# A recurrent attention and four-expert kernel: the first group's first layer in f32r parts for three of its four experts

## The chip, the cores and the metric

The kernel runs on one core of a Trainium2 chip. The metric is the device time of one execution in microseconds (us); the time before is the median of three runs. A profile is one more execution, with its own time.

## The reference

Two blocks follow each other. The first is a gated linear recurrence per batch and head, with 4 batches, 8 heads, 768 steps and head size 48; the second multiplies each of the 3072 tokens (384 values) by four experts' two layers and adds the results with normalised weights.

```python
for t in range(S):
    state = alpha[:, :, t, :, None] * state + np.einsum('bhd,bhe->bhde', k[:, :, t], v[:, :, t])
    y[:, :, t] = np.einsum('bhd,bhde->bhe', q[:, :, t], state)
...
x = np.ascontiguousarray(attn_out.transpose(0, 2, 1, 3)).reshape(B * S, H * D)
...
p = domain_probs / (domain_probs.sum(-1, keepdims=True) + 1e-09)
for e in range(E):
    h = np.maximum(x @ w1[e], 0.0)
    out += p[:, e:e + 1] * (h @ w2[e])
```

All data are float32. w1 is 384 x 1024 and w2 1024 x 384 for each of the four experts.

## The kernel before, in words

**Units and groups.** The sequence is cut into six blocks of 128 steps. A block of one batch is a unit, 24 in all; a unit's attention yields 128 tokens of x. Units are gathered into groups (L117): the first group has two units (256 tokens), four groups have four, the last has two. For each group the experts' layers run one expert after the other (`tasks`, L119): `up` is the first layer, one call for each of the eight 128-wide hidden tiles (called fc 0 to 7 below), `down` the second layer, and `add_up` (L863) weights and sums.

**f32 and f32r.** TensorE takes a plain float32 product in several passes, an f32r product in one, at less precision. From the second group on each operand of a product is therefore split into three f32r parts (a rounded top, a sum and a rest scaled up), and a product is three f32r products, one for each part. For w1 and w2 this is `split_piece` (L241): ACT makes the top part, DVE the two others (L250, L252, L253), and POOL's queue writes all three to DRAM (`kept`, L256), from where later groups load them (L214). A weight matrix of an expert is cut into four such pieces, so pieces 0 to 3 belong to the first expert, 4 to 7 to the second, and so on. For x it is `split_x` (L720): ACT makes the top of all three 128-row slices in step 0, DVE the two other parts of one slice in each of the steps 1 to 3.

**The first group** does not use parts. Its `up` multiplies the plain f32 x by the plain f32 w1 (L769), with the relu on ACT (L771); its `down` is plain f32 too (L847, 16 matmuls of each expert for each of the two units). Its raw x lies in the third part of the tile xT (L446 and L667). Beside that, the pieces of w1 are split for the later groups: for the second to fourth expert two pieces are queued at the start of one of the calls of `down` of the expert before (L814), the two others after the hidden tiles 2 and 4 of its own `up` (`SPLIT_AT`, L203). The first expert runs in two halves of 128 tokens, since the second unit's x comes later.

**Background and order.** `background` (L258) issues the steps of queued splits: a top part on ACT, at the next call its DVE operations. The order on every engine is thus the order in which the program text issues things. The attention of coming units runs beside the layers as a generator that is stepped at times that a planner deals out (`deal`, L895); `advance` (L944) adds the estimated cost of each layer's step (`cost`, L889) to a clock and steps what is due.

**A unit's steps** that the prediction speaks of: transposes on TensorE (tp, L287) with their copies on ACT (L494 and L502); L507, L508 and L520 on DVE; then seven levels, of which each has copies of q on ACT (qb, L541), products of q, decay and k on DVE (L548, L550, L560) and a copy of k on ACT (L559); near (L593); score products on TensorE (sc, L567) and masked copies on DVE (L577); the far products (L623) with their copies (L636); lat (L640); yps (L662), which gives x (copied by L675); and the state (sps, L697; L705 to L708).

The tile pools set when buffers come free: the parts of w1 have four buffers (`AHEAD`, L200), so the fourth next piece waits until the older one's write to DRAM has been done and its readers are through.

Of the kernel before, what the change touches and what calls it, by code (L numbers as in the profile page):

```python
# [20 lines left out]
def kernel(  # L21
# [37 lines left out]
    nc = tc.nc  # L59

    B, H, S, D = q.shape
    E, DM, F = moe_w1.shape
    P = 128
# [5 lines left out]
    KC = DM // P  # L69
    FCH = F // P  # L70
    NT = B * P
    NQ = 4
# [74 lines left out]
    hidden = {}  # L147
    finish = deque()
    making = deque()
    splitting = []  # L150
    stores = deque()
    late = deque()
# [47 lines left out]
    AHEAD = 4  # L200


    SPLIT_AT = [{1: 2, 4: 3}, {1: 0, 3: 1, 5: 2, 7: 3}]  # L203
    BESIDE = [{2: 0, 3: 1, 4: 2, 5: 3}, {1: 2, 2: 3}]

    def load_piece(l, i, beside=False):
# [34 lines left out]
    def split_piece(l, i):  # L241
        gi, k = divmod(i, E * NQ)
        whole = wt[l][i]
        if i >= E * NQ:
            w = wt[l][i] = wts.tile([P, 3, KC * QF], F32R, name="w2", bufs=NQ)
        else:
            w = wts.tile([P, 3, KC * QF], F32R, name="w1", bufs=AHEAD)
        top, both, rest = (w[:, part] for part in range(3))

        nc.scalar.activation(out=top, in_=whole, func=ACT.Copy, scale=LIFT)  # L250
        yield
        nc.vector.tensor_sub(rest, whole, top.bitcast(F32))  # L252
        nc.vector.scalar_tensor_tensor(out=both, in0=rest.bitcast(F32), scalar=4096.0, in1=whole,  # L253
                                       op0=ALU.mult, op1=ALU.add)
        if (gi, k // NQ) != (1, 0):
            nc.gpsimd.dma_start(out=kept[l][k], in_=w.bitcast(F32))  # L256

# [32 lines left out]
    def first_unit(fill, other):  # L290
# [153 lines left out]
        flat_v = rv.rearrange("p h d -> p (h d)")  # L444
        work.tile([P, 96], F32, name="space", bufs=1)
        xTs[0] = work.tile([P, 3, KC, NT], F32R, name="xT", bufs=1)  # L446
        xraws[0] = xTs[0][:, 2].bitcast(F32)
        terms = [[] for _ in range(P // QUAD)]
        for c in range(KC):
            for j, strip in enumerate(terms):  # L450
# [9 lines left out]
            nc.scalar.copy(out=xraws[0][:, :, HALF * s:HALF * (s + 1)], in_=y)  # L460
        next_k(6)
        return rest_of_first(AT, KTs[6], rv)

    def rest_of_first(AT, KT, rv):
        nc.scalar.copy(out=AT, in_=turned(lambda p: KT[:, p, :]))
        yield
        sps = ps.tile([P, NP, 2, D], F32, name="sps", tag="w")
        for p in range(NP):
            nc.tensor.matmul(sps[:, p], lhsT=AT[:, p], rhs=rv[:, 2 * p:2 * p + 2, :D], start=True, stop=True)
        for i in range(2):  # L470
            rows = slice(HD * i, HD * (i + 1))
            nc.vector.tensor_copy(out=sts[units[0][1]][rows, :, i, :], in_=sps[rows, :, i, :])
        load(2, "v")
        yield

    def attention(u):
# [171 lines left out]
        def result():  # L648
            yps = ps.tile([P, KC, P], F32, name="yps", tag="w")
            strips = [[] for _ in range(P // QUAD)]  # L650
            for c in range(KC):
                for j, strip in enumerate(strips):
                    p, part = divmod(len(strips) * c + j, 3)
                    terms = [(flat_st[:, p, QUAD * part:QUAD * (part + 1)], QT[:, p, :])] if cb > 0 else []
                    for i in range(2):
                        if part != 2 * (1 - i):
                            at = VD * (2 * p + i) + QUAD * part - D * i
                            terms.append((flat_v[:, at:at + QUAD], lat[:, 2 * p + i, :]))
                    strip += [(c, n == 0, n == len(terms) - 1, *term) for n, term in enumerate(terms)]
            for turn in zip(*strips):  # L660
                for j, (c, begins, ends, lhsT, rhs) in enumerate(turn):
                    nc.tensor.matmul(yps[QUAD * j:QUAD * (j + 1), c, :], lhsT=lhsT, rhs=rhs,  # L662
                                     start=begins, stop=ends)
            gi, slot = place[cb, b]
            if slot == 0:
                if gi == 0:
                    xTs[gi] = work.tile([P, 3, KC, NT], F32R, name="xT", bufs=1)  # L667
                    xraws[gi] = xTs[gi][:, 2].bitcast(F32)
                elif gi < LAST:
                    xraws[gi] = work.tile([P, KC * NT + PAD], F32, name="x_raw", bufs=1)[:, :KC * NT]  # L670
                    xraws[gi] = xraws[gi].rearrange("p (c n) -> p c n", n=NT)
                else:
                    xraws[gi] = []
            if gi < LAST:
                nc.scalar.copy(out=xraws[gi][:, :, slot * P:(slot + 1) * P], in_=yps)  # L675
            else:

                xraws[gi].append(AT)
                nc.scalar.copy(out=AT[:, :KC, :], in_=yps)
# [33 lines left out]
    def x_part(gi, part, kc):  # L713
        n = len(groups[gi]) * P
        if gi < LAST:
            return xTs[gi][:, part, kc, :n]
        t, i = divmod(part * KC + kc, NP * P // n)
        return xTs[gi][t].rearrange("p a n -> p (a n)")[:, i * n:(i + 1) * n]

    def split_x(gi, step):  # L720

        n = len(groups[gi]) * P
        if step == 0 and gi < LAST:
            xTs[gi] = work.tile([P, 3, KC, NT], F32R, name="xT", bufs=1)
        elif step == 0:

            xTs[gi] = [work.tile([P, NP, P], F32R, name="KT", bufs=5) for _ in range(5)]
        for kc in range(KC) if step == 0 else [step - 1]:
            parts = [x_part(gi, part, kc) for part in range(3)]
            pieces = [(xraws[gi][:, kc, :n], parts)] if gi < LAST else                 [(raw[:, kc, :], [part[:, s * P:(s + 1) * P] for part in parts])  # L730
                 for s, raw in enumerate(xraws[gi])]
            for x, out in pieces:
                if step == 0:
                    nc.scalar.activation(out=out[0], in_=x, func=ACT.Copy, scale=TRIM)
                else:
                    split_rest(x, out)


    def up(gi, e, fc, slots=None):
# [17 lines left out]
            for k in range(NQ):  # L757
                load_piece(0, (e + 1) * NQ + k)
        col = slice(f * P, (f + 1) * P)
        if gi > 0:  # L760
            w = wt[0][i].rearrange("p t (c f) -> p t c f", f=QF)[:, :, :, col]
        else:
            w = wt[0][i].rearrange("p (c f) -> p c f", f=QF)[:, :, col]
        parts = [hidden[c][:, part, f, lo:hi] for part in range(3)]
        whole = parts[2].bitcast(F32)
        one = ps.tile([P, NT], F32, name="one", tag="g", bufs=4)[:, :hi - lo]
        if gi == 0:
            for kc in range(KC):
                nc.tensor.matmul(one, lhsT=w[:, kc], rhs=xraws[gi][:, kc, lo:hi],  # L769
                                 start=(kc == 0), stop=(kc == KC - 1))  # L770
            nc.scalar.activation(out=whole, in_=one, func=ACT.Relu)  # L771
        else:
            for part in (1, 2, 0):
                for kc in range(KC):
                    nc.tensor.matmul(one, lhsT=w[:, part, kc], rhs=x_part(gi, part, kc),  # L775
                                     start=(part == 1 and kc == 0), stop=(part == 0 and kc == KC - 1))
            nc.scalar.activation(out=parts[0], in_=one, func=ACT.Relu, scale=TRIM)  # L777
            while finish:
                hidden_rest(*finish.popleft())
            finish.append((one, parts))  # L780
# [27 lines left out]
    def down(gi, e, slots, between):  # L808
# [2 lines left out]
        first = first_piece(gi, e)  # L811
        tiles = range(FCH)
        if gi == 0 and e < E - 1 and slots[0] == (e == 0):
            making.extend(split_piece(0, first + NQ + k) for k in range(2))  # L814
        if gi == 0 and e == E - 1 and slots[0] == 1:
            making.extend(split_piece(1, first + NQ + k) for k in range(NQ // 2))
        while fresh(gi, e) and (making or splitting):
# [71 lines left out]
    def cost(layer, gi, e):  # L889
        n = len(groups[gi]) / 4  # L890
        if layer == 0:
            return 2.1 * n if gi > 0 else 2.6 * n
        return 4.1 if gi > 0 else 5.4

    def deal():  # L895
# [54 lines left out]
    with tc.manual_schedule():  # L950
# [46 lines left out]
        for (gi, e), after in zip(tasks, [*tasks[1:], (None, None)]):  # L997
            rest = gi == e == 0
            for fc in range(FCH):
                up(gi, e, fc, slice(1, len(groups[0])) if rest else None)  # L1000
                advance(cost(0, gi, e) / (2 if rest else 1))
            each = len(groups[gi]) if gi > 0 else 1
            turns = [range(k, k + each) for k in range(rest, len(groups[gi]), each)]
            for k, slots in enumerate(turns):

                between = deque()
                if after[1] == 0:

# [36 lines left out]
```

## Time and profile before

| | us |
|---|---|
| median of three runs | 1033.85 (1030.1 to 1035.3) |
| profiled execution, its own time | 1027.61 |
| its span, first to last instruction | 1025.7 |
| TensorE matmul busy | 998.4 (97%) |
| DVE busy | 702.4 (68%) |
| ACT busy | 438.7 (43%) |
| first group's first layer, TensorE (L769) | 46.2 in 240 passes, 20.4 to 145.0 |

The time of the profiled execution holds the span and a little around it. Busy time counts an engine's instructions, with matmul ends modelled. The chain of waits goes back from the last instruction to what released each step, and so names what ended last in each stretch. A group of instructions is given as line, engine, operation and tiles; L769 appears twice as often as the program issues it, since a plain f32 matmul is recorded as two. Stretches list the busy time of each engine between two times.

### The profile page before, as it was taken

The page shows a single profiled execution, that of the slowest core. Times are in us where ns is not written, and L with a number is a line of the kernel's source. Part 1 is how long each engine was busy: PE and PEld are TensorE (multiplying, and loading weights), DVE is VectorE, ACT ScalarE, POOL GpSimd, SP SyncE. Part 2 cuts the span into 40 slices and gives each one's busy share as a digit, 9 for nine tenths or more (in the row PEclk, how much of TensorE's full clock was granted, in tenths as well). Part 3 has the DMA queues.
Part 4 walks back from the last instruction along what each step waited for, and adds up shares of the span by engine and source line. Part 5 has one row for each costly group of instructions (what it writes and reads, how often), then busy time and mean ns, then how long its engine had stood idle before and what let it go on. Part 6 is the DMA issues. An engine that isn't in the chain of part 4 may idle for free.

```text
span 1025.7 us, 21120 instructions
## 1 busy us (share of the span) xinstructions
PE 998.4 (97%) x8564; PEld 886.7 (86%) x8564; DVE 702.4 (68%) x1430; ACT 438.7 (43%) x961; POOL 36.1 (4%) x79
## 2 busy tenths in 40 slices
PE   8889999999999999999999999999999999999998
PEld 7667777988888799898898898888988989898998
DVE  5698879687979868677767666885877743434343
ACT  5687666365354444335443415444454332211111
POOL 2010000000000100000000000000000000000000
PEclk9999999999999999999999999999999999999999
DMA  9499699398988999789889759786796454454531
GB/s 214 135 387 282 201 359 338 107 337 265 322 284 249 317 296 330 284 253 317 287 259 334 235 214 385 263 274 261 212 365 250 170 205 184 185 195 174 221 149 47
DMA packets 155632, 260.19 MB, mean 254 GB/s; under 512 B 95216, under 2 KB 132464, under 8 KB 133520
## 3 DMA queue, kind: packets, MB, share of 16 engines
q1 hardware_dynamic: 149072, 216.44, 63.7%
q0 software_dynamic: 6016, 42.08, 10.2%
q8 instruction: 68, 1.11, 0.4%
q10 hardware_dynamic: 448, 0.33, 0.1%
q14 instruction: 28, 0.23, 0.1%
HBM read 216.35 MB, written 42.47 MB: 252 GB/s over the span
## 4 chain that ended last, share of the span: by engine, by line
PE 81%; DVE 11%; ACT 4%; issue 2%; DMA 0%; POOL 0%; DVEq 0%; SPq 0%; ACTq 0%; POOLq 0%
PE ops L847 35%; PE one L775 31%; PE sc L567 5%; PE yps L662 3%; PE one L769 2%; PE tp L287 2%; DVE w L252 2%; ACT qb L541 2%; DVE hT L805 1%; DVE hT L800 1%; DVE near L577 1%; DVE QT L548 1%; PE sps L697 1%; DVE w L253 1%; PE far L623 1%
## 5 line engine op out<-in xcount | busy, mean ns | idle before, releaser
L847 PE MATMUL ops<-w,hT 128*128 128x384 f32 x2112 | 381.8, 339 | 9.4 <-ACT hT L777 6.7
L847 PEld LDWEIGHTS ops<-w,hT 128*128 128x128 f32 x2112 | 366.4, 189 | 15.6 <-ACT hT L777 8.9
L775 PE MATMUL one<-xT,w 128*128 128x512 f32 x1440 | 342.8, 394 | 0.8 <-DVE acc L875 0.8
L775 PEld LDWEIGHTS one<-xT,w 128*128 128x128 f32 x1440 | 266.8, 188 | 58.3 <-DVE acc L875 1.2
L777 ACT ACTIVATE hT<-one 128x512 fp32r<-128x512 f32 (+1 forms) x192 | 107.9, 562 | 343.4 <-PE one L775 318.7
L800 DVE SCALAR_TENSOR_TENSOR hT<-one,hT 128x512 fp32r<-128x512 f32 (+1 forms) x192 | 122.3, 645 | 105.2 <-ACT hT L777 104.8
L541 ACT COPY qb<-QT 64x256 f32<-64x256 f32 x322 | 131.1, 407 | 88.7 <-DVE QT L518 44.9
L548 DVE TENSOR_TENSOR QT<-QT,AT 128x256 f32<-128x256 f32 x158 | 66.7, 422 | 85.9 <-ACT qb L541 85.1
L805 DVE SCALAR_TENSOR_TENSOR hT<-hT 128x512 fp32r<-128x512 f32 (+1 forms) x192 | 112.8, 640 | 0.1
L577 DVE COPY_PREDICATED near<-masks,sc 128x256 f32<-128x256 uint8 x138 | 73.9, 536 | 41.5 <-PE sc L567 38.1
L567 PEld LDWEIGHTS sc<-qb,KT 128*64 128x64 f32 x2208 | 69.7, 138 | 7.3 <-issue 5.7
L567 PE MATMUL sc<-qb,KT 128*64 128x64 f32 x2208 | 74.0, 223 | 0.9 <-ACT qb L541 0.9
L875 DVE SCALAR_TENSOR_TENSOR acc<-ops,p_all,acc 128x384 f32<-128x384 f32 x66 | 40.0, 614 | 42.8 <-PE ops L847 42.8
L560 DVE TENSOR_TENSOR KT<-KT,AT 128x256 f32<-128x256 f32 x161 | 67.4, 418 | 0.0
L559 ACT COPY KT<-KT 128x256 f32<-128x256 f32 x138 | 57.5, 416 | 3.3
L769 PE MATMUL one<-xT,w 128*128 128x256 f32 (+1 forms) x240 | 46.2, 340 | 0.4 <-ACT xT L460 0.4
L847 PE MATMUL ops<-hT 128*128 128x384 f32 x128 | 46.2, 494 | 0.0
L550 DVE TENSOR_TENSOR AT<-AT 128x256 f32<-128x256 f32 (+1 forms) x138 | 39.1, 284 | 4.7
L769 PEld LDWEIGHTS one<-xT,w 128*128 128x128 f32 x240 | 37.7, 191 | 4.9 <-ACT xT L460 0.6
L884 POOL DMA_DIRECT2D out_dram<-acc x22 | 11.9, 540 | 673.7 <-DVE acc L875 673.7
L662 PE MATMUL yps<-lat,rv 128*32 128x128 f32 x736 | 33.1, 273 | 1.6 <-ACT lat L640 1.6
L775 PE MATMUL one<-KT,w 128*128 128x256 f32 x288 | 34.6, 279 | 0.0
(119 smaller groups left out, 709.1 us busy)
## 6 DMA issues: line engine op xcount, KB each, us to landing
w<-kept SPq DMA_DIRECT2D x140, 1152.0 KB, 8.8
kept<-w POOLq DMA_DIRECT2D x32, 1152.0 KB, 8.7
hT<-in_moe_w_dram SPq DMA_DIRECT2D x36, 384.0 KB, 5.9
w<-in_moe_w_dram SPq DMA_DIRECT2D x16, 384.0 KB, 5.8
rv<-in_v_dram SPq DMA_DIRECT2D x24, 192.0 KB, 9.3
out_dram<-acc POOLq DMA_DIRECT2D x22, 192.0 KB, 6.4
rk<-in_k_dram SPq DMA_DIRECT2D x14, 192.0 KB, 6.1
rq<-in_q_dram SPq DMA_DIRECT2D x14, 192.0 KB, 3.0
```

The source lines that it names most:

```text
L541: nc.scalar.copy(out=qb[rows, :, i, :].rearrange("p a (b r) -> p a b r", r=m), in_=qv[rows])
L548: nc.vector.tensor_mul(qv, qv, spread(dv[:, :, :, 0], m))
L560: nc.vector.tensor_mul(new[:, :, :, 0, :], old[:, :, :, 0, :], spread(halved(decs[li])[:, :, :, 1], m))
L567: nc.tensor.matmul(out[HALF * s:HALF * (s + 1), 2 * p:2 * p + 2, :], lhsT=KTs[li][:, p, HALF * s:HALF * (s + 1)], rhs=qbs[li][:, p, :, QUA ...
L577: nc.vector.copy_predicated(near.rearrange("p a (b two r) -> p a b two r", two=2, r=m)[:, :, :, 1, :], mk.unsqueeze(1).broadcast_to([P, H, ...
L662: nc.tensor.matmul(yps[QUAD * j:QUAD * (j + 1), c, :], lhsT=lhsT, rhs=rhs, start=begins, stop=ends)
L769: nc.tensor.matmul(one, lhsT=w[:, kc], rhs=xraws[gi][:, kc, lo:hi], start=(kc == 0), stop=(kc == KC - 1))
L775: nc.tensor.matmul(one, lhsT=w[:, part, kc], rhs=x_part(gi, part, kc), start=(part == 1 and kc == 0), stop=(part == 0 and kc == KC - 1))
L777: nc.scalar.activation(out=parts[0], in_=one, func=ACT.Relu, scale=TRIM)
L800: nc.vector.scalar_tensor_tensor(out=low, in0=x, scalar=0.0, in1=top.bitcast(F32), op0=ALU.max, op1=ALU.subtract)
L805: nc.vector.scalar_tensor_tensor(out=dif, in0=low.bitcast(F32), scalar=-4096.0, in1=top.bitcast(F32), op0=ALU.mult, op1=ALU.add)
L847: nc.tensor.matmul(sums[slot], lhsT=h, rhs=w, start=(n == begins[slot]), stop=(n == ends[slot]))
```

## The change

In the first group, the first layer of the second, third and fourth expert is computed in three f32r parts like that of the later groups. Raw x lies in a tile of its own (`x_raw`), and is split into the three parts of xT beside the second unit's call of `down` of the first expert; the parts begin 16 elements into their rows (`SHIFT`). The parts of w1 are read from the tiles in which `split_piece` makes them (`ready`), and `up` issues background steps until its piece has been issued. Three pieces instead of two are queued at the start of `down`, and the fourth after the first hidden tile of `up`. The relu still makes the whole f32 hidden value on ACT. The planner's cost of such a layer is lowered from 2.6 to 2.1 for a full group.

```diff
-    SPLIT_AT = [{1: 2, 4: 3}, {1: 0, 3: 1, 5: 2, 7: 3}]
+    SPLIT_AT = [{0: 3}, {1: 0, 3: 1, 5: 2, 7: 3}]
+    SHIFT = 16
...
+        if i < E * NQ and l == 0:
+            ready[i] = w
...
-        xraws[0] = xTs[0][:, 2].bitcast(F32)
+        xraws[0] = x_raw()
...
+    def x_raw():
+        t = work.tile([P, KC * NT + PAD], F32, name="x_raw", bufs=1)
+        return t[:, :KC * NT].rearrange("p (c n) -> p c n", n=NT)
...
-                if gi == 0:
-                    xTs[gi] = work.tile([P, 3, KC, NT], F32R, name="xT", bufs=1)
-                    xraws[gi] = xTs[gi][:, 2].bitcast(F32)
-                elif gi < LAST:
-                    xraws[gi] = work.tile([P, KC * NT + PAD], F32, name="x_raw", bufs=1)[:, :KC * NT]
-                    xraws[gi] = xraws[gi].rearrange("p (c n) -> p c n", n=NT)
-                else:
-                    xraws[gi] = []
+                xraws[gi] = x_raw() if gi < LAST else []
...
-            return xTs[gi][:, part, kc, :n]
+            return xTs[gi][:, part, kc, SHIFT * (gi == 0):][:, :n]
...
-        if gi > 0:
-            w = wt[0][i].rearrange("p t (c f) -> p t c f", f=QF)[:, :, :, col]
+        in_parts = gi > 0 or e > 0
+        if in_parts and gi == 0:
+            while i not in ready:
+                background()
+        if in_parts:
+            w = (wt[0] if gi > 0 else ready)[i].rearrange("p t (c f) -> p t c f", f=QF)[:, :, :, col]
...
-        if gi == 0:
+        if not in_parts:
             for kc in range(KC):
                 nc.tensor.matmul(one, lhsT=w[:, kc], rhs=xraws[gi][:, kc, lo:hi],
                                  start=(kc == 0), stop=(kc == KC - 1))
-            nc.scalar.activation(out=whole, in_=one, func=ACT.Relu)
...
-            making.extend(split_piece(0, first + NQ + k) for k in range(2))
+            making.extend(split_piece(0, first + NQ + k) for k in range(3))
...
-            return 2.1 * n if gi > 0 else 2.6 * n
+            return 2.1 * n if gi > 0 or e > 0 else 2.6 * n
...
+                if rest:
+                    between.extend((at, lambda step=step: split_x(0, step))
+                                   for step, at in enumerate((0.0, 0.25, 0.5, 0.75)))
```

More of the change, by code (lines that the diff above doesn't have):

```diff
@@ L149 @@
     making = deque()
+    ready = {}
     splitting = []
@@ L722, in split_x @@
         n = len(groups[gi]) * P
-        if step == 0 and gi < LAST:
+        if step == 0 and 0 < gi < LAST:
             xTs[gi] = work.tile([P, 3, KC, NT], F32R, name="xT", bufs=1)
-        elif step == 0:
+        elif step == 0 and gi == LAST:
             xTs[gi] = [work.tile([P, NP, P], F32R, name="KT", bufs=5) for _ in range(5)]
@@ L776, in up @@
                                      start=(part == 1 and kc == 0), stop=(part == 0 and kc == KC - 1))
+        if gi == 0:
+            nc.scalar.activation(out=whole, in_=one, func=ACT.Relu)
+        else:
             nc.scalar.activation(out=parts[0], in_=one, func=ACT.Relu, scale=TRIM)
```

## The prediction

> **What bounds the kernel now.** I read the page first. TensorE is busy 97% of the span, so a change that takes matmul time away looks like a gain. But the change touches only the first group, so the question is what ends last there. The stretches of 20 us say it (after the time: busy us and instruction count of PE, PEld, DVE, ACT, POOL, then granted clock, DMA share, GB/s):
>
> ```profile
> 40.00:60.00 20.00, 19.03 (x167) 15.48 (x166) 15.63 (x28) 15.06 (x34) 2.27 (x4) 1.00 0.74 243
> 60.00:80.00 20.00, 16.72 (x196) 13.72 (x195) 18.62 (x38) 16.24 (x40) 2.12 (x4) 1.00 1.04 383
> 80.00:100.00 20.00, 20.00 (x205) 14.81 (x204) 17.02 (x38) 13.25 (x30) 1.06 (x2) 1.00 0.98 303
> ```
>
> The reader is to see that in 60 to 80, the stretch of the second expert's first layer, DVE is the full engine and PE is not. The chain of waits confirms it: from 51.9 to 78.0 it runs almost wholly over DVE and ACT (two stretches of it; the last line is where PE takes over):
>
> ```profile
> 55.64 0.88 DVE w L252
> 56.52 0.02 issue
> 56.54 0.96 DVE w L253
> 57.49 0.60 DVE near L593
> ...
> 62.12 0.96 DVE w L252
> 63.10 0.96 DVE w L253
> ...
> 69.47 0.68 DVE QT L520
> 70.17 0.43 ACT qb L541
> ...
> 77.96 0.69 PE sc L567 x16
> ```
>
> From 78 to 160 it is mostly PE, with one DVE stretch from 101 to 111. After 160 PE is full (40.00 of 40 us in 160 to 200), and from the second group's first layer on the instructions of both kernels stand in the same order on each engine. So I take what the first group gains or loses by 160 to be carried unchanged to the end.
>
> **The matmuls: 5.8 us less PE work.** Per 128-wide hidden tile the old layer issues 3 plain f32 matmuls, recorded as 6 passes; the new one 9 f32r matmuls of the same width. Both have a row, the second in the last group, which has 256 tokens too:
>
> ```profile
> 140.00 5.37 PE L769 MATMUL one<-xT,w 128*128 128x256 f32 x24
> 145.21 2.74 PE L847 MATMUL ops<-hT 128*128 128x384 f32 x8
> ...
> 954.80 8.64 PE L775 MATMUL one<-KT,w 128*128 128x256 f32 x72
> 963.28 8.49 PE L847 MATMUL ops<-w,hT 128*128 128x384 f32 x48
> ```
>
> Start to start, four old tiles take 145.21 - 140.00 = 5.21, 1.30 each; eight new ones take 963.28 - 954.80 = 8.48, 1.06 each. Eight tiles of three experts: 24 x 0.24 = 5.8 us, 1.9 an expert. Reading x 16 elements into its rows has no row of its own; I take nothing for it, and at worst the whole 5.8 is lost. The Trainium skill (FP8 and Floating Point Precision, TensorE Precision Notes) counts a true f32 product as four passes, so three parts would be worth a quarter of 24 x 1.30, 7.8 us; by that the result below would be 2 us lower. The trace has six passes against nine matmuls at 1.30 to 1.06, and I go by it.
>
> **What is added on DVE and ACT.** The 16 splits of w1 were made before too (to be kept in DRAM); they only move. New is the split of x: three ACT copies of 128x256 at 0.38 (row L771) and six DVE operations of 128x256 at 0.42 by the rows L548 and L560, about 0.75 a pair start to start: 3 x 0.75 = 2.25 us (2.0 by half the pair at 512, 1.33; 2.5 by the mean durations). The separate tile for raw x adds no instruction. The queue of SP has the same transfers with one load of q a few places earlier, POOL the same 16 writes: nothing taken.
>
> **The new wait: second expert.** In the changed order the first part of this expert's w1 (piece 4) is split on DVE only after this list, counted from 55.56 in the old trace, the end of level 2 of the running attention unit: x pair 0.75, near 0.61, x pair 0.75, piece 3 1.85, level 3 0.91, two masked copies 1.29, x pair 0.75, level 4 0.89, two masked copies 0.79, piece 4 itself 1.90. That is 10.5 us. Before it, ACT makes the three x copies ahead of the copy qb that level 2 waits for, 1.0 us. So piece 4 is there at 55.6 + 1.0 + 10.5 = 67.1. PE is done with the second layer of the first expert at about 59.3 (57.84 before; qb and with it the last score products come 1.0 later, and three instead of one L847 matmul pairs stand behind them). **PE waits some 7.8 us at the first hidden tile**, where it waited for nothing.
>
> Behind that tile's matmuls on PE stand the transposes of the next unit, which are not missed yet. But ACT has its relu next in its queue, and behind the relu the top part of piece 6 and qb of level 5. Relu ends at 68.7, the copy of piece 6 at 69.5, qb at 70.3; DVE, done with piece 5 at 69.0, waits 1.3 for it. Then level 5, piece 6, L507 and L508, and piece 7, which stood behind the next unit's first level before (72.32 in the old trace, where DVE was waiting on ACT anyhow), now stands ahead of that unit's L520: 1.9 us. Piece 7 also needs the buffer of piece 3, whose write to DRAM can start at 60.5 and lands 8.6 later, at 69.1: before ACT comes to it at 71.6, so hidden; if not, each us late goes to the chain.
>
> **The clock.** An idle PE has a price in this trace. Around two waits of 1.28 and 1.10 us in the second group (columns as above):
>
> ```profile
> 310.00:312.00 2.00, 0.99 (x6) 0.67 (x4) 1.97 (x3) 0.37 (x1) 0.00 (x0) 1.00 0.94 315
> 312.00:314.00 2.00, 0.63 (x2) 0.38 (x3) 1.25 (x3) 1.67 (x4) 0.53 (x1) 0.86 1.01 404
> 314.00:316.00 2.00, 2.00 (x7) 2.00 (x8) 1.95 (x5) 1.96 (x6) 0.00 (x0) 0.50 1.08 416
> 316.00:318.00 2.00, 2.00 (x11) 2.00 (x10) 1.97 (x4) 1.16 (x3) 0.00 (x0) 0.79 0.97 363
> ```
>
> 2.4 us of waiting put the granted clock to a half until about 3 us after PE had work again. With 7.8 us of waiting I expect the same: the first tile takes 2.1 instead of 1.06, its relu comes 1.1 later, and with it qb and level 5; 1.2 us on the chain. The Trainium skill (TensorE: Matmul & The Clock Gate, Part 1) gives the rule behind it, half clock after an idle window of some 3.4 us and back after as long a busy one; the trace agrees, with its 3 us at 0.50.
>
> **The sum.** The next unit's L520 and qb, from which the chain goes on, come later by 2.25 (x on DVE) + 1.0 (x on ACT) + 1.3 (qb behind relu) + 1.9 (piece 7 ahead) + 1.2 (clock) = 7.7 us. In the second layer of that expert DVE no longer waits for TensorE ahead of L520 (it waited 1.17 for the sum at 85.81): 0.3 back. Third expert: the first tiles have their pieces in time, but from the end of level 2 to level 5 of the unit DVE now has three splits, 11.5 us by the rows above (3 x 1.9, near 0.6, levels 3 and 4 1.8, masked copies 2.1, sum 0.55, L705 0.75), where it had 9.9 (level 2 ended at 95.6, level 5 began at 105.54) with one split and 2.08 of waiting in it and another split, 1.9, just ahead of level 2. So level 5 and qb of the far products (PE was at them at 107.56) come no earlier, PE waits there some 2.5 us with one tile fewer left behind it, and the 1.9 saved is gone. Fourth expert: its last two splits follow the second sum of the third expert's second layer, so they are ready 0.6 + 1.9 = 2.5 and 4.4 us after that layer; PE comes to them after four tiles, yps and sps, 4.2 + 1.7 + 0.9 = 6.8, and 8.9 us. No wait, 1.9 gained. 7.7 - 0.3 + 0 - 1.9 = **5.5 us slower**.
>
> The profiled execution took 1027.61 us (span 1025.7), so 1033.1 by its own count. It lies 6.2 under the median of the runs shown, 1033.85; there the forecast is 1039.
>
> **The rivals.**
> - *The split keeps up* (faster): piece 4 is ready when PE comes to it, and all the PE time is gained: 1033.85 - 5.8 = 1028. It decides at the first tile of the second expert: DVE would have to have piece 4 ready by 59.3, 7.8 us before the end of my list. For it: the top part is there early, and PE is 97% busy overall. Against it: the order on DVE, and no idle time on DVE between 51.9 and 75. Chance 0.12.
> - *The loss is made good later:* DVE idled 1.17, 0.50, 2.08 and 0.34 ahead of L875 and L548 between 84 and 107; if all 4.1 us take up the delay: +1.4, 1035. For it: DVE's work is the same as before there. Against it: those waits are for ACT and PE, which come later as well. Chance 0.2.
> - *It is worse:* in the fourth expert too the splits end late, the 1.9 is not gained, and the wait at the far products costs clock again, half of 3 us: +5.5 + 1.9 + 1.5, 1043. For it: two splits stand back to back at the end of DVE's list there. Chance 0.2.
> - *As forecast:* 0.45, between 1036 and 1042; 0.03 for anything else.
>
> The range leaves out the first rival and a little above the third: 1030 to 1045. Some 0.5%, 5.2 us, is what a measurement can tell from no change, so the border for slower is 1039.0, about my own number: half of the forecast and the worse case give 0.46 with the rest; faster is the first rival, 0.12; between them 0.42.
>
> **What would show it.** Right: an idle PE of 7 to 8 us ahead of the first tile of the parts' line around 60 to 67, ended by DVE's second split operation, with a granted clock near 0.5 behind it; a first tile of the second group that starts 5 to 6 us after 159.2. Tiles of 1.06 us in the fourth expert; a wait ahead of the far products in the third. Wrong: no PE wait over 3 us in that place (the first rival), or a second group that starts as early as before (the second).

## The result, and the profile after

| | before | after |
|---|---|---|
| median, us | 1031.5 (6 runs, 1028.93 to 1035.3) | 1040.37 (6 runs, 1039.96 to 1043.4) |
| profiled execution, its own time | 1027.61 | 1040.03 |
| its span | 1025.7 | 1038.1 |
| TensorE matmul busy | 998.4 | 996.4 |
| mean granted clock | 0.998 | 0.993 |

The changed kernel takes 1.0086 times the time of before, 95% interval 1.007 to 1.0102: **8.9 us more**. The profiled execution of before lies under all six runs of its median, so the 12.4 us between the two profiles are not the measure.

The three stretches of 20 us from the changed kernel's profile (columns as in the prediction: PE, PEld, DVE, ACT, POOL, granted clock, DMA share, GB/s):

```profile
40.00:60.00 20.00, 17.45 (x156) 13.62 (x156) 14.73 (x27) 14.20 (x33) 1.74 (x3) 1.00 0.73 240
60.00:80.00 20.00, 12.83 (x113) 12.63 (x114) 16.36 (x31) 9.74 (x22) 2.66 (x5) 0.74 0.85 313
80.00:100.00 20.00, 17.93 (x203) 13.33 (x202) 15.41 (x38) 15.99 (x39) 0.53 (x1) 1.00 0.67 195
```

In 60 to 80 TensorE does 3.9 us less than before (16.72), and DVE, which was full at 18.62, is now at 16.36: both wait, and the clock is down to 0.74. The chain of waits of the same kernel (start, us, what) has the reason:

```profile
56.50 0.35 DVE xT L275
...
58.70 0.88 DVE w L254
...
65.17 0.96 DVE w L254
...
66.16 0.97 DVE w L255
...
67.17 2.29 PE one L779 x9
...
86.69 0.69 PE sc L575 x16
```

The list of DVE work leads from x (L275) over piece 3 (58.70) to piece 4, which ends at 67.13; TensorE's first tile starts then. The last score products ahead of the second layer stand at 86.69; before, they stood at 77.96. TensorE's own timeline of the changed kernel, with the idle time ahead of each group in brackets:

```profile
57.38 2.20 PE L854 MATMUL ops<-hT 128*128 128x384 f32 x6
67.17 2.29 PE L779 MATMUL one<-xT,w 128*128 128x256 f32 x9 [7.59 <-DVE w L255]
...
69.97 2.27 PE L779 MATMUL one<-xT,w 128*128 128x256 f32 x9
...
72.74 1.35 PE L779 MATMUL one<-xT,w 128*128 128x256 f32 x9
```

A stop of 7.59 us, then two tiles of 2.3 us instead of 1.3. Stretches of 2 us there show the granted clock:

```profile
62.00:64.00 2.00, 0.00 (x0) 0.00 (x0) 1.90 (x6) 1.44 (x3) 0.00 (x0) 0.65 1.11 429
64.00:66.00 2.00, 0.00 (x0) 0.00 (x0) 1.97 (x5) 0.00 (x0) 0.00 (x0) 0.50 0.83 351
...
70.00:72.00 2.00, 2.00 (x11) 2.00 (x10) 0.62 (x3) 1.97 (x5) 0.05 (x1) 0.50 0.99 369
72.00:74.00 2.00, 2.00 (x16) 2.00 (x15) 1.97 (x3) 1.95 (x5) 0.00 (x0) 0.79 0.93 376
```

And in the last expert of the group TensorE has a wait that was not there before:

```profile
146.93 5.55 PE L779 MATMUL one<-xT,w 128*128 128x256 f32 x45
152.35 1.53 PE L854 MATMUL ops<-hT 128*128 128x384 f32 x4
156.31 1.56 PE L854 MATMUL ops<-hT 128*128 128x384 f32 x4 [2.43 <-DMA hT<-in_moe_w_dram]
...
168.68 3.65 PE L779 MATMUL one<-xT,w 128*128 128x512 f32 x14
```

The second layer waits 2.43 us for its weights from DRAM (plain w2 lies in a free part of the hidden tiles, hence hT). On the chain, which counts from where a step is released, the second group's first tile starts at 169.13 instead of 159.22: 9.9 us late. From there to 300 us every landmark is late by the same 9.9. Later the delay moves between 8.5 and 12.3, among other things with half-clock stretches that only one of the two profiles has (before at 313 to 317, after at 370 to 373).

**How profiles are compared below.** The first 45 us differ by up to 3 us between executions of the same order of work, so all times below count from the first state products (sps) after 40 us of their own profile. The landmarks: the next unit's first product on DVE (L520, in the changed kernel L528), the second expert's first tile, the end of the score products ahead of its second layer, the fourth expert's first tile, and the first 512-wide tile of the second group. The landmarks of a row come from one execution, its ratio from the medians, each beside executions of the kernel before that were taken with it; the two need not agree to the us.

| kernel | unit | expert 2 | scores' end | expert 4 | group 2 | ratio to before, 95% |
|---|---|---|---|---|---|---|
| before | 25.3 | 13.7 | 34.5 | 87.1 | 114.6 | 1 |
| after | 32.6 | 22.8 | 43.0 | 96.4 | 124.3 | 1.0086 (1.007 to 1.0102) |
| e1, second expert plain | 30.3 | 14.5 | 39.5 | 91.7 | 118.1 | 1.0022 (1.0009 to 1.0035) |
| e2, x earlier | 30.3 | 20.5 | 40.9 | 94.3 | 121.8 | 1.0051 (1.0034 to 1.0068) |
| e3, later loads | 32.6 | 22.8 | 42.8 | 96.2 | 125.9 | 1.0066 (1.0049 to 1.0083) |
| e4, wait filled | 31.7 | 22.8 | 41.0 | 94.4 | 119.4 | 1.0048 (1.0033 to 1.0063) |
| e5, w2 early | 32.7 | 22.8 | 42.2 | 95.6 | 120.6 | 1.0059 (1.0036 to 1.0082) |
| e6, urgent piece first | 25.1 | 14.7 | 38.4 | 91.8 | 120.6 | 1.0112 (1.0076 to 1.0147) |
| e7, e2 + e5 + e6 | 20.4 | 14.8 | 34.0 | 87.4 | 112.5 | 1.0014 (0.9998 to 1.0031) |
| e9, fourth expert alone | 25.3 | 13.7 | 36.8 | 94.2 | 119.2 | 1.0044 (1.003 to 1.0059) |
| e10, second expert alone | 32.6 | 21.0 | 41.8 | 94.6 | 123.5 | one run |
| e11, e9 with the old cost | 25.3 | 13.7 | 35.9 | 88.0 | 113.9 | 0.9979 (0.9964 to 0.9995) |
| e12, e11 with x earlier | 26.0 | 14.4 | 35.2 | 87.9 | 113.9 | 0.998 (0.9965 to 0.9994) |

One execution of e6 and one of e8 ran near 1400 us in a disturbed state of the chip, e8's profiled one among them; e8 therefore has no landmarks.

### The profile page after: what moved, and what is told of

It reads as the page before. It is cut to its first block, busy times and chain, and to the rows that moved or that the text cites. A ratio compares the mean times of both kernels' runs of the same rounds, so it can differ in the third digit from the quotient of the medians.

```text
span 1038.1 us, 21276 instructions
## 1 busy us (share of the span) xinstructions
PE 996.4 (96%) x8636; PEld 887.5 (85%) x8636; DVE 704.5 (68%) x1436; ACT 439.8 (42%) x964; POOL 36.1 (3%) x79
## 3 DMA queue, kind: packets, MB, share of 16 engines
q0 software_dynamic: 6016, 42.08, 10.2%
## 4 chain that ended last, share of the span: by engine, by line
PE 76%; DVE 12%; DMA 5%; ACT 4%; issue 2%; SPq 0%; DVEq 0%; ACTq 0%
PE ops L854 32%; PE one L779 32%; PE sc L575 5%; PE yps L670 3%; DVE hT L812 2%; PE tp L291 2%; ACT qb L549 1%; DMA w<-kept 1%; DVE w L254 1%; DVE near L585 1%; DMA hT<-in_moe_w_dram 1%; DMA rv<-in_v_dram 1%; PE sps L698 1%; DVE QT L556 1%; DVE w L255 1%
## 5 line engine op out<-in xcount | busy, mean ns | idle before, releaser
L779 PE MATMUL one<-xT,w 128*128 128x512 f32 (+1 forms) x1656 | 374.2, 381 | 8.4 <-DVE w L255 7.6
L779 PEld LDWEIGHTS one<-xT,w 128*128 128x128 f32 x1656 | 295.2, 189 | 67.3 <-DVE w L255 8.2
L556 DVE TENSOR_TENSOR QT<-QT,AT 128x256 f32<-128x256 f32 x158 | 66.7, 422 | 95.0 <-ACT qb L549 94.4
L779 PEld LDWEIGHTS one<-KT,w 128*128 128x128 f32 x288 | 34.4, 188 | 0.0
L854 PEld LDWEIGHTS ops<-hT 128*128 128x128 f32 x128 | 22.2, 190 | 14.0 <-DMA hT<-in_moe_w_dram 3.0
## 6 DMA issues: line engine op xcount, KB each, us to landing
rv<-in_v_dram SPq DMA_DIRECT2D x24, 192.0 KB, 10.1
```

What stands on the lines that cost most here:

```text
L556: nc.vector.tensor_mul(qv, qv, spread(dv[:, :, :, 0], m))
L854: nc.tensor.matmul(sums[slot], lhsT=h, rhs=w, start=(n == begins[slot]), stop=(n == ends[slot]))
```

## The experiments

All edits are made to the changed kernel.

**e1: the second expert plain again**, with the lists of DVE and ACT left as they are. Raw x lies in a free buffer, and the second expert's planner cost is 2.6 again.

```diff
-        in_parts = gi > 0 or e > 0
+        in_parts = gi > 0 or e > 1
```

> The second expert's first layer is plain f32 again (raw x read from a free third of a weight tile, the planner's cost as before for it); third and fourth expert stay in parts, and every split stands where the change put it. Theory A (the list on DVE and ACT holds back the next attention unit: x pairs 2.25, x copies 1.0, piece 7 ahead 1.9; the stopped TensorE adds the rest): no TensorE wait near 60, the last score products ahead of the second expert's second layer end about 5 us later than before (before 78.6, changed 87.4), so about 84. Theory B (all of the loss is the stopped TensorE and its clock): they end at 78.6 as before. Total: A some 3 to 4 us under the changed kernel, B 8 to 9 under it.

TensorE's timeline of e1:

```profile
60.40 1.56 PE L854 MATMUL ops<-hT 128*128 128x384 f32 x4
61.79 1.46 PE L774 MATMUL one<-w 128*128 128x256 f32 x6
```

No stop at the first tile, and yet the next unit's copy comes at 30.3, exactly 5.0 after that of before (25.3). DVE works from 58.5 on without a gap ahead of it, so this is the list alone, as theory A had it: the x pairs, the x copies and piece 7 ahead of the unit, which the prediction had put at 2.25 + 1.0 + 1.9 = 5.15. The stop, the relu behind it and the clock add 2.3 at the copy (32.6). At the score products they add 3.5 (43.0 against 39.5), though e1 has a half clock of its own ahead of these (0.50 in 72 to 76, beside waits of 2.42 and 1.46 us).

**e2: x split one step ahead of each of the first four tiles of the first expert's second half.**

```diff
+                if rest and fc < 4:
+                    split_x(0, fc)
                 up(gi, e, fc, slice(1, len(groups[0])) if rest else None)
...
-                if rest:
-                    between.extend((at, lambda step=step: split_x(0, step))
-                                   for step, at in enumerate((0.0, 0.25, 0.5, 0.75)))
```

> The changed kernel with x of the first group split beside the first tiles of the first expert's second half, where DVE had waited 6.0 us (37.6 to 43.6 before). Theory A: DVE's list ahead of piece 4 is 2.25 shorter and ACT's 1.0, so TensorE's wait falls from 7.6 to about 4.3, and the second group starts some 3.3 us earlier (about 166, changed 169.1). Theory B (the place of x's split does not matter, the order of w1's pieces does): the wait stays above 6.5.

The stop shrinks from 7.59 to 5.21 us, the copy comes 2.3 earlier, the second group 2.5, of which 0.4 is a shorter wait for w2 (1.98 us against 2.43). The place of the x split is thus worth some 2.3 us of the 3.25 that the prediction had for it; about 0.9 is paid in the new place, where the unit before has its copy at 6.0 instead of 5.1.

**e3: the second group's loads of w1**, which the fourth expert's first layer issues, moved behind it.

```diff
-                for k in range(2 if e == E - 1 and c > 1 else 0):
-                    load_piece(0, E * NQ + 2 * (c - 2) + k)
...
+        if gi == 0 and e == E - 1 and slots[0] == 0:
+            for k in range(NQ):
+                load_piece(0, E * NQ + k)
```

> The changed kernel with the second group's four loads of w1 issued at the start of the fourth expert's second layer instead of after its tiles 5 and 7. The changed kernel waits 2.4 us there for the plain w2 of the fourth expert. Theory A (those loads share the DMA engines with it): the wait goes, the second group starts at about 166.7 instead of 169.1, if its own first pieces are still in time. Theory B (the loads of w2 can only start when the second layer of the expert before is done, and the shorter first layer no longer covers them): the wait stays at 1.5 to 2.5.

The wait for w2 stays, 2.73 us: theory B. These loads do not cause it. In this execution the second group starts 1.6 later all the same. TensorE never waits for the moved loads; the wait for w2 is 0.3 longer, and behind it the clock drops:

```profile
158.00:160.00 2.00, 2.00 (x8) 1.46 (x7) 0.03 (x1) 0.53 (x1) 0.00 (x0) 0.59 1.08 365
160.00:162.00 2.00, 2.00 (x8) 0.66 (x8) 0.00 (x0) 0.46 (x2) 0.00 (x0) 0.55 1.13 398
```

The medians do not show a loss beside the changed kernel (1.0066, whose interval overlaps with that of 1.0086).

**e4: TensorE kept busy in the stop** with 18 needless matmuls of 128x192 on the identity, ahead of the second expert's first tile.

```diff
+        if gi == 0 and e == 1 and fc == 0:
+            busy = ps.tile([P, NT], F32, name="one", tag="g", bufs=4)
+            for _ in range(18):
+                nc.tensor.matmul(busy[:, :P + HALF], lhsT=ident, rhs=ident_all[:, :P + HALF], start=True, stop=True)
```

> The changed kernel with 18 matmuls of 128x192 on constant data (some 6 us of work that nobody reads) on TensorE ahead of the second expert's first tile, where it waits 7.6 us. Theory A (the half clock costs 1.2 us on the chain): the granted clock stays at 1.0 there, the first tile takes 1.1 instead of 2.3, and the second group starts 1 to 2 us earlier than 169.1. Theory B (the clock costs nothing, DVE decides): the clock is better and the second group starts at 169.

TensorE's timeline of e4:

```profile
61.61 6.01 PE L768 MATMUL one<-ident 128*128 128x192 f32 x36
69.38 1.33 PE L783 MATMUL one<-xT,w 128*128 128x256 f32 x9 [1.76 <-DVE w L255]
```

The first tile starts at the same 22.8, but takes 1.33 instead of 2.29 us, and the clock stays at 1.00. The copy comes 0.9 earlier, the score products 2.0. So the half clock of the changed kernel's profile costs 2.0 us on the chain, where the prediction had 1.2. The further gain at the second group (119.4) is that this execution has no wait for w2.

**e5: w2 of the fourth expert loaded early**, at the start of the third expert's second layer, into buffers that are free by then (`shared[k][:, 0]`), instead of at its own first layer.

```diff
-        if gi == fc == 0 and begins:
+        if gi == fc == 0 and begins and e < E - 1:
...
+        if gi == 0 and e == E - 2 and slots[0] == 0:
+            for k in range(NQ):
+                w = wt[1][(E - 1) * NQ + k] = shared[k][:, 0].bitcast(F32)
+                nc.sync.dma_start(
+                    out=w.rearrange("p (c d) -> p c d", d=DM),
+                    in_=moe_w2[E - 1].rearrange("(c p) d -> p c d", p=P)[:, k * FPQ:(k + 1) * FPQ])
```

> The changed kernel, with the fourth expert's plain w2 loaded at the start of the third expert's second layer, into a free third of the tiles that hold raw w1 (it was loaded at the start of the fourth expert's first layer). Theory A (the shorter first layer left the load uncovered, 11.4 us against 12.2 to land): no TensorE wait for DMA at the fourth expert's second layer, and the second group starts 2.5 to 3 us earlier against the first state products than in the changed kernel (124.3 there, so about 121.5; 114.6 before). Theory B (DMA engines are full there in any case): the wait moves to other loads and the start stays within 1 us.

TensorE's timeline of e5, to be laid beside that of the changed kernel above:

```profile
147.47 5.55 PE L779 MATMUL one<-xT,w 128*128 128x256 f32 x45
152.86 2.74 PE L860 MATMUL ops<-w,hT 128*128 128x384 f32 x8
...
166.41 5.91 PE L779 MATMUL one<-xT,w 128*128 128x512 f32 x24
```

The second layer runs through, and from the fourth expert's first tile to the second group it is 25.0 us instead of 27.9 (before: 27.5). The gain of the fourth expert is real, and the wait for w2 took it back. (Of the 2.5 us against before, 0.9 only moved: two groups of transposes that stood between its tiles now stand ahead of the first one.)

**e6: the urgent pieces first.** Pieces 4 to 7 are split during the second half of the first expert's first layer, ahead of pieces 0 to 3, which nobody needs soon and which now go between the later experts' tiles; the second expert's w1 is loaded correspondingly sooner. The numbers in the table are now pieces.

```diff
-    SPLIT_AT = [{0: 3}, {1: 0, 3: 1, 5: 2, 7: 3}]
+    SPLIT_AT = [{1: 4, 3: 5, 5: 6, 7: 7}, {3: 0, 5: 1}, {0: 11}, {0: 15, 2: 2, 4: 3}]
...
-        if gi == 0 and e < E - 1 and slots[0] == (e == 0):
+        if gi == 0 and 0 < e < E - 1 and slots[0] == 0:
```

> The changed kernel, with the second expert's w1 loaded at the start and its four pieces split where those of the first expert were; the first expert's pieces, which only later groups need, are split beside the first layers of the second and the fourth expert. x is split where the change put it. Theory A (the order of the splits on DVE stops TensorE): no wait above 2 us at the second expert's first tile, the score products ahead of its second layer end 2 to 3 us earlier than before (32 after the first state products; 34.5 before, 43.0 changed), the second group starts at 112 to 113 if the load of w2 is in time. Theory B (DVE has too much in that stretch whatever the order): they end at 38 or later.

TensorE's timeline of e6:

```profile
64.69 1.29 PE L779 MATMUL one<-xT,w 128*128 128x256 f32 x7 [3.35 <-DVE xT L275]
```

The first tile starts 8.1 earlier, but still stops after two matmuls: now the x pairs are late, where I had expected no stop. The score products end 4.6 earlier, the second group starts 3.7 earlier. Yet e6 is the slowest of all, 1038.78 to 1046.51. The view of waits of e6 from 165 to 420 us (us in total, times, longest) has one that neither kernel has:

```profile
PE far L631 <- ACT qb L549: 4.7, 1, 4.7
```

It stands 11 us into the second group's first layer. The kernel before has its other waits there too, but not this one. The chain of waits leads back from it to the top part of a split (L252) of the second group's w2 on ACT, which waits for its load from DRAM; the unit's copies stand behind it in ACT's queue. ACT's timeline of e6:

```profile
170.56 0.85 ACT L252 ACTIVATE w<-hT 128x768 fp32r<-128x768 f32 x1 [8.08 <-DMA hT<-in_moe_w_dram]
```

The kernel before waits 2.06 us at this split, the changed one not at all. In e6 the four loads land 13.5 to 16.8 us after issue (changed kernel: 10.1 to 11.1), and two writes of kept pieces that the new order has left for the end of the group begin just ahead of them, at 150.36 and 153.31; that these slow the loads is argued from their times and was not tried by itself. Behind the wait e6 is 12.0 us later than before, 6.0 at the first tile of the second group. The score products at 38.4 are what theory B said (38 or later).

**e7: e6, e2 and e5 together.**

> The three together: splits in the order of need, x split early, w2 of the fourth expert loaded early. Theory A: the second unit's L520 comes at about 20 after the first state products (25.3 before, 32.6 changed), the second group starts at about 108 (114.6 before), and the total is some 6 us under the kernel before. Theory B (the third expert's three splits and the attention units' chain take it back): the second group starts at 112 or later, and the total is within 3 us of before.

TensorE's timeline of e7, at the second expert and in the second group:

```profile
59.84 2.20 PE L860 MATMUL ops<-hT 128*128 128x384 f32 x6
61.58 1.52 PE L779 MATMUL one<-xT,w 128*128 128x256 f32 x9
...
168.29 0.66 PE L631 MATMUL far<-qb,KT 128*64 128x128 f32 x8 [2.43 <-ACT qb L549]
```

No stop, and the second group starts at 112.5, 2.1 earlier than before and 11.8 earlier than in the changed kernel (the three edits alone gave 2.5, 3.7 and 3.7). It is the only kernel that brings all three experts in parts without loss in the first group. But 9 us later it waits 2.43 in the same place as e6, behind the same split (ACT waits 4.75 us for its load), the clock drops after it (0.61 in 168 to 172), and the lead is gone: by 198 us it is 1.8 behind the kernel before. In the end it is level, 1032.42 against 1031.71.

**e8 and e10: the second expert alone in parts** (e10 is e8 once more, for its profile).

```diff
-        in_parts = gi > 0 or e > 0
+        in_parts = gi > 0 or e == 1
```

> Parts in the second expert alone; third and fourth expert are plain f32 (raw x from a free third of a weight tile, planner's cost as before for them); splits stand where the change put them. Theory A (all of the loss up to the score products is the second expert's, the third gains nothing, the fourth gains 1.9 and loses it and more by the wait for w2): score products end at 43, the second group starts at about 123, with no wait for w2. Theory B (the third and fourth expert cost more in parts than they save): it starts at 120 or earlier.

> The kernel of e8 once more, for its profile. Only the second expert is in parts. Theory A: the next unit's first DVE copy L528 at 32.6 and the score products' end at 43.0 after the first state products, as in the changed kernel; the third expert's first layer neither gains nor loses; the fourth is plain, so that no w2 load is late, and the second group's first wide tile starts at 122 to 124 (changed kernel 124.3, before 114.6). Theory B (third and fourth expert in parts lose by themselves): it starts at 120 or earlier.

e8 took 1041.68 (ratio 1.0091, 1.0065 to 1.0117), as long as the changed kernel; e10's one run 1042.51. In e10 the stop is 5.75 us, with the unit's steps in another order; the copy comes at the same 32.6, and the second group at 123.5 against 124.3: the third and fourth expert in parts bring next to nothing in the changed kernel. One thing I had not expected, in e10's timeline of TensorE:

```profile
158.71 0.91 PE L854 MATMUL ops<-hT 128*128 128x384 f32 x2 [1.11 <-DMA hT<-in_moe_w_dram]
```

Here the fourth expert's first layer is plain and takes its old 14.0 us (140.43 to 154.42), and w2 is still late. So the shorter first layer is only part of why the cover is gone.

**e9: the fourth expert alone in parts**, w2 early as in e5, the old order of splits for the second and third expert, x split beside the second slot of the second expert's second layer, and the planner's cost lowered for the fourth alone.

```diff
-        in_parts = gi > 0 or e > 0
+        in_parts = gi > 0 or e == E - 1
...
-            return 2.1 * n if gi > 0 or e > 0 else 2.6 * n
+            return 2.1 * n if gi > 0 or e == E - 1 else 2.6 * n
...
-    SPLIT_AT = [{0: 3}, {1: 0, 3: 1, 5: 2, 7: 3}]
+    SPLIT_AT = [{1: 0, 3: 1, 5: 2, 7: 3}, {1: 2, 4: 3}, {1: 2, 4: 3}, {0: 3}]
```

> Only the fourth expert of the first group is computed in parts; the second and third are plain again with their old order of splits, x is split beside the second slot of the second expert's second layer (where DVE had over 1 us of waiting in the kernel before), and w2 of the fourth expert is loaded into a place of its own early, as in e5. Theory A (the loss comes from DVE's and ACT's list ahead of the second expert, the gain is only to be had in the fourth, and w2's load is what took it back): nothing moves up to the second expert's second layer; three pairs of x on DVE cost there 0 to 2.25 us, and the fourth expert brings 1.9 to 2.4; the first wide tile of the second group starts 0 to 2.4 us earlier than before against the first state products (114.6 before, so 112.2 to 114.6), ratio 0.997 to 1.000. Theory B (moving x or the lowered cost by itself makes the loss): second group 2 us or more later than before, ratio 1.002 or more.

Theory A fails, since the score products are 2.3 late; the signs of theory B come (the second group 4.6 later, 1.0044). The fourth expert takes 25.0 us from its first tile to the second group, as in e5, for 27.5 before, but 7.1 are lost ahead of it, 2.3 of them by the score products and the rest in the plain third expert (0.9 of that are the two groups of transposes that moved, as in e5). TensorE's timeline of e9 shows a place, with a granted clock of 0.50 behind it (110 to 112):

```profile
108.98 0.66 PE L291 MATMUL tp<-ident,sk 128*128 128x128 f32 x4 [2.88 <-ACT AT L502]
```

**e11 and e12: which of the two, x or the cost.** e11 is e9 with the cost left as it was before:

```diff
-            return 2.1 * n if gi > 0 or e == E - 1 else 2.6 * n
+            return 2.1 * n if gi > 0 else 2.6 * n
```

e12 is e11 with the x split of e2.

> As e9 (only the fourth expert in parts, x split beside the second slot of the second expert's second layer), with the planner's cost of that layer left at 2.6. Theory A (what e9 lost came from the three x pairs on DVE standing ahead of the third expert's copies): as e9, the first tile of the fourth expert at 93 to 95 after the first state products (94.2 in e9, 87.1 before), ratio 1.003 to 1.006. Theory C (the lowered cost shifts the attention steps to worse places): the first tile of the fourth expert at 87 to 90, ratio 0.998 to 1.001.

> As e11, with x split one step ahead of each of the first four tiles of the first expert's second half, as in e2. Theory A: x there cost the next unit's first copy about 0.9 in e2 and e7 (6.0 against 5.1), the fourth expert gives 2.4 back: the second group's first wide tile 112 to 114 after the first state products (114.6 before), ratio 0.997 to 1.000. Theory D (whatever is added to DVE before 130 us costs more than its own length): the fourth expert's first tile 90 or later (87.1 before), ratio 1.001 or more.

The same wait in TensorE's timeline of e11:

```profile
106.77 0.66 PE L291 MATMUL tp<-ident,sk 128*128 128x128 f32 x4 [0.68 <-ACT AT L502]
```

It is back to the 0.68 us that before has. One number in the planner, 2.1 instead of 2.6 for eight tiles of one expert, is worth 5.3 us at the second group and 7.1 in the medians (1037.94 beside 1032.43 for before, 1030.68 beside 1032.28): it moves the unit's steps among the tiles. So theory C of e11 and theory A of e12 hold. The x split costs little in either place (the fourth expert's first tile is 0.9 and 0.8 late). **e11 and e12 are the only kernels faster than before**, by 0.2% (1030.68 and 1030.66 against 1032.28), with intervals that leave out 1.

## Why the prediction was right, and where it was not

**The direction and the place: right. The nearness of the time: in part luck.** 1039 was said, 1040.37 measured. But the effect itself was undersized: 5.5 us in the sum, 8.9 in the medians, 9.9 at the second group. The 1039 started from 1033.85, the median of the three runs shown; six runs of the kernel before have 1031.5, and 5.5 on top of that is 1037.0. Of the signs named, the stop, the half clock, tiles of 1.06 us (five take 5.42) and the wait ahead of the far products came; a second group 5 to 6 us late did not, it is 9.9.

**The matmuls: right.** In the fourth expert of the changed kernel it is 11.6 us instead of 14.0 from first tile to second layer (140.78 to 152.35, 131.21 to 145.21), 2.4 less, where the sum had 1.9. But the steps between the tiles are not the same. Two groups of transposes that stood there before (the first two lines) now stand ahead of the first tile (the last two):

```profile
132.50 0.60 PE L287 MATMUL tp<-ident,sq 128*128 128x128 f32 x4
134.24 0.60 PE L287 MATMUL tp<-ident,KT 128*128 128x128 f32 x4
...
139.56 0.60 PE L291 MATMUL tp<-ident,KT 128*128 128x128 f32 x4
139.99 0.60 PE L291 MATMUL tp<-ident,sq 128*128 128x128 f32 x4
```

They are 0.9 us, start to start. In e11 and e12, which keep the old cost, they stand between the tiles as before, and the layer takes 12.4 us (133.52 to 145.90 in e11): the matmuls alone are worth 1.6.

**The list on DVE and ACT: right.** Piece 4 ended at 67.1 as worked out; TensorE waited 7.59 for 7.8; L528 came at 77.01 against 69.46, 7.55 later for 7.7. e1 measures the list without the stop as 5.0 for 5.15.

**The clock: the mechanism right, the size a matter of the execution.** A half clock followed, in the changed kernel's profile for 10.2 us (62.6 to 72.8, worked out from the shares in the stretches), 4.6 of it while TensorE stood still. It slowed two tiles, not one, and e4 puts it at 2.0 us for 1.2. In the profile of e5, which has the same order up to there and the same stop of 7.59 us, the half clock lasted 6.8 us (65.6 to 72.4, from the shares in these two stretches of it):

```profile
64.00:66.00 2.00, 0.00 (x0) 0.00 (x0) 1.93 (x7) 0.86 (x2) 0.00 (x0) 0.89 1.10 444
...
72.00:74.00 2.00, 2.00 (x17) 2.00 (x17) 1.20 (x4) 1.96 (x7) 0.00 (x0) 0.91 0.98 366
```

There the score products are 1.2 later than in e4 (42.2 against 41.0), just what was forecast. The Trainium skill (TensorE: Matmul & The Clock Gate, Part 1) has windows of 3413 ns that run freely; three of them are 10.2 us and two are 6.8, and the traces agree. The prediction took the two waits of the kernel before as agreeing with the rule of an idle window; it is the 3.4 us of half clock behind them that do, while the waiting came to 2.4 us only.

**What the longer half clock brought: a copy behind the fifth tile.** At the score products the delay was 8.5, not 7.7 - 0.3: the next unit's first qb stands on ACT behind the relu of the fifth tile, as the ACT timeline of the changed kernel shows.

```profile
78.40 0.38 ACT L782 ACTIVATE hT<-one 128x256 f32<-128x256 f32 x1 [2.39 <-PE one L779]
78.79 0.86 ACT L549 COPY qb<-QT 64x256 f32<-64x256 f32 x2
```

L528 was done at 77.69 and qb began at 78.79: 1.1 us. I had looked at the relu of the first tile and at no other. In e4, at full clock, the same qb waits for L528 alone:

```profile
78.98 0.86 ACT L549 COPY qb<-QT 64x256 f32<-64x256 f32 x2 [0.45 <-DVE QT L528]
```

So this 1.1 us is no term beside the clock's: with the 0.9 at the copy it makes the 2.0 that e4 measures.

**Third expert, no gain: right.** TensorE waited 0.92 and 0.96 us in it for ACT (2.5 in one place was said), and its far products came at 116.06 for 107.56, still 8.5 late.

**The step that failed: "nothing taken" for the queues.** The transfers are the same in number, but not in time. SP issued the fourth expert's four loads of w2 in this way in the changed kernel:

```profile
141.08 5.17 SPq L239 DMA_DIRECT2D hT<-in_moe_w_dram  x4
```

and before:

```profile
131.64 3.33 SPq L237 DMA_DIRECT2D hT<-in_moe_w_dram  x4
```

Before, the four were issued in 3.33 us, landed 6.8 to 8.6 us after issue, and 14.0 us of first layer lay over them. Now they take 5.17 us to issue, beside kept writes that start at 141.42, 144.40 and 146.26 (before: 131.17, 138.20, 147.00), land 11.1 to 12.6 us after issue, and have 11.6 us of first layer. The chain of waits follows one of them for 12.24 us. e5 measures what it costs here: with w2 elsewhere the fourth expert and its second layer take 25.0 us for 27.9. It is not the same in every execution: with the same loads e2 waits 1.98 us, e3 2.73, and e4 not at all. e3 excludes the loads behind it. e10 shows that the shorter layer is not all of it. That the bunched writes are the rest is argued from their times; no run moved them alone.

**The sum as it ran:** 7.3 at the unit's copy, 1.2 more at the score products, nothing in the third expert, less 1.6 for the fourth's matmuls, plus 2.8 in its second layer: 9.7 by the table, 9.9 by the chain. (The 9.3 at the fourth expert's first tile have the 0.9 of the transposes in them.) The forecast had 7.4, 0, -1.9 and 0.

**The rivals.** *The split keeps up* fell at 67.17; e7 shows what it would have taken, the moves of e6 and e2 together. *Made good later* fell: the delay was 8.5 at the score products and 9.7 at the second group; in between it was smallest at the third expert's state products, 6.7. *Worse* had the right sum, 8.9, with the wrong mechanism: the fourth expert did gain, and the far products cost no clock.

**What stays open.** The planner's lowered cost is part of the change, and I had read it as part of the order and never priced it. e9 and e11 show that it can be worth 5 us in one order of work; the changed kernel itself with the old cost was not tried.

## What to carry to other kernels

A faster matmul helps only where TensorE ends last: look up, tile by tile, who makes its operands, and what stands ahead of them in that engine's order. Where a layer becomes shorter, ask which load was hidden under it, and start that load earlier (e5). Where a planner deals out work by estimated costs, a corrected estimate is a change of its own and wants a run of its own (e9 against e11).

## What the runs showed of the chip

- The same stop of 7.59 us held the clock at a half for 10.2 us in one execution (the changed kernel) and for 6.8 in another (e5). The spell after two waits of 1.28 and 1.10 us in the kernel before was 3.4 us (313.4 to 316.8, by the shares 0.86, 0.50 and 0.79 in the prediction). 18 matmuls on the identity, with 1.76 us of idling left, kept it at 1.00 (e4).
- One wait of 2.43 us can drop the clock (e7, 0.61 in 168 to 172), and one of the same 2.43 us need not: after the wait for w2 in the changed kernel the clock stays at 1.00, after the 2.73 us of the same wait in e3 it drops.
- The same x split, three ACT copies and three DVE pairs, costs some 2.3 us more in one place of the order than in another (e2 against the changed kernel), and under 1 us in two places where only the fourth expert uses it (e11, e12).
